# A gated linear-attention block: seven products for block 1's keys and queries, another sequence of the first half, late features for three blocks' queries, fewer GpSimd scale operations

## The chip, the cores and the metric

The kernel runs on one core of a Trainium2 chip. Its time is the device time of one execution in microseconds (us); lower is better. The core has a matrix engine (TensorE, PE in the profile), a vector engine (VectorE, DVE), an activation engine (ScalarE, ACT), a general engine (GpSimd, POOL) and DMA queues, here those of SyncE (SP) and of GpSimd. Each engine works through its own instructions in the order of the program and waits on semaphores for the others.

## The reference

```python
x = A_x                                   # 1 x 2048 x 512
xn = _layernorm(x, axis=-1)
s = _A_ref(xn, A_wqkv, A_wo)              # linear attention
g = _silu(_B_ref(xn, B_w1, B_w2, B_w3, B_w4))
return x + s * g

def _A_ref(x, wqkv, wo):                  # H = 32 heads of Dh = 16
    phi = lambda t: jnp.where(t > 0, t + 1, jnp.exp(t)) + 1e-6
    pq, pk = phi(q), phi(k)
    kv = jnp.einsum("bhsd,bhse->bhde", pk, v)
    z = jnp.einsum("bhsd->bhd", pk)
    num = jnp.einsum("bhqd,bhde->bhqe", pq, kv)
    den = jnp.einsum("bhqd,bhd->bhq", pq, z)[..., None] + 1e-6
    o = num / den
    return o.reshape(B, S, D) @ wo

def _B_ref(x, w1, w2, w3, w4):
    h = _gelu(_layernorm(x, axis=-1) @ w1)
    # four quarters of h shifted by +1, -1, +2, -2 rows, concatenated
    x1 = x + hs @ w2
    return x1 + _gelu(_layernorm(x1, axis=-1) @ w3) @ w4   # F = 1376
```

All of it is float32.

## The kernel before

**Tiling.** The 2048 rows are 4 blocks (b) of 512 rows, and each block is 4 tiles (i = 4b to 4b + 3) of 128 rows. The inner dimension of 512 is four chunks (c) of 128. A product in full precision is made of three products of rounded parts: each operand is split into a high part (`...h`, rounded) and a low part (`...l`, the rest), and high x high, high x low and low x high are added in PSUM (`products`, line 475). So every operand costs one rounding (mostly on ScalarE) and one subtraction (VectorE) ahead of its first product (`rounded`, line 483).

**First half.** For every tile: keys, their features (`feature_k`, line 774), the gram product of keys and normalized rows (`gram`, line 866, accumulated over all 16 tiles in four PSUM banks), queries and their features. For every block: the mixing products with W1 (`mixer`, tiles `h`, `ht`), the transforms of their result (`forms`) and the products with W2 (`mix2`, tiles `pam`, `pbm`, `pem`, `o`).

Keys and queries of a tile are made in one of two ways. `key` and `query` (lines 789 and 810) project one tile from the plain transposed rows: 12 products of 512 columns each, and a VectorE step that takes the mean out. `keys_queries(b, j)` (line 839) makes keys and queries of two tiles together in seven block products in place of eight (Winograd's scheme): 42 products of 512 columns for four projections. It needs the centred rows and four sums of them (`make_u`, line 672, for which the means of the block come back from DRAM as one broadcast row, `um`) and four sums of the key and query weights (`forms_kq`, line 819, named "T" in the sequence). Before, blocks 0 and 1 take the first way and blocks 2 and 3 the second.

**Queries' features.** phi needs max and exp of the query. `feature_q` (line 802) makes relu(q), exp(-relu(-q)) on ScalarE (two Relu and one Exp), stores the first part in DRAM (`pqd`) and adds the second by an accumulating DMA from GpSimd's queue. `turn_q` (line 1168) fetches the features in the second half, normalizes them on VectorE and sends them through a transposition.

**Scales.** The row statistics (`mv1`, `mv2`) become 1/sqrt(var + eps) by a power on GpSimd (`power`, line 598). The operations around it (add eps; the negative scale `ns1`; minus mean times scale, `nm1` and `nm2`; the variance of the second norm, `pu`) are GpSimd's too (`scale_x`, `scale_u`, `mixed`).

**Second half.** Per block, pairs of W3 blocks (`up_pair`, seven products, Gelu), the products with W4 (`down`, tiles `acc`), the attention output (`attend_pair`, tiles `pas`, `pbs`, `pes`) and the gate.

**What sets the order.** All operations are recorded in a plan (`Plan`, line 87). The order in which TensorE's operations are recorded gives each a nominal time from a table of costs; `deadlines` counts back from these to a due time of every other operation. `emit` (line 268) then places the operations of all engines in simulated time, with costs for each kind, and writes the program in that order; TensorE may take an operation up to 12 us ahead of its turn. `SOONER` (line 1510) moves the due times of single operations by quarters of a microsecond. So the sequence of the first half, `ORD` (lines 1382 to 1390), sets TensorE's order: "q", "k" are projections, ("kq", b, j) seven products, "g" a gram, "mix" a block's mixing, "m2" two tiles' W2 products, "w1" the centring and splitting of W1 (`w1_for`; its column mean comes from TensorE as `w1m`), "st" row statistics, "u" the centred forms, "x" scaled rows, "a" and "h" the broadcast rows (`abc`) and edges for mixing.

Of the kernel before, what the change touches and what calls it, by code (L numbers as in the profile page):

```python
# [13 lines left out]

P = 128
SCARCE = 3.0
EPS = 1e-5
# [69 lines left out]
class Plan:  # L87
# [70 lines left out]
    def act(self, out, src, func, scale=1.0, bias=None, total=None):  # L158
        nc = self.nc
        psum = out.tile.psum or src.tile.psum  # L160
        lat = .17 + out.n / 1200 + (.09 if isinstance(scale, View) else 0) + (0 if psum else .02)
        table = 0 if func == AF.Exp else 1 if func in (AF.Gelu_apprx_tanh, AF.Tanh) else None

        def emit():
            kw = {} if bias is None else {"bias": bias.get()}
            if total is not None:
                kw["accum_out"] = total.get()
            nc.scalar.activation(out.get(), src.get(), func, scale=get(scale), **kw)  # L168

        self.add("ACT", lat - .1, lat, [src, scale, bias], [out] + ([] if total is None else [total]), emit, table=table)  # L170

    def vec(self, eng, out, reads, emit, pair, scalars=0):
        views = [v for v in reads if isinstance(v, View) and v.n > 4]
        sb = not any(v.tile.psum for v in views + [out])
        n = max([v.n for v in views] + [out.n])
        if eng == "POOL":
            lat = (.3 if n <= 8 else .15 + n / (435 if pair else 1000))
# [219 lines left out]
def linear_attn_gated_by_mixer(  # L397
# [30 lines left out]
    SUMS = "DVE"  # L428
    SOON = {"T": 30.0, "u": 5.0}
    AHEAD = 70.0, 50.0, 30.0, 10.0, 0.0  # L430
# [14 lines left out]
    def piece(name, dt=F32):  # L445
        return pl.new("p", name, dt, PIECE)[:, :512]
# [151 lines left out]
    def power(out, src, n):  # L598
        nh = nhalf[:, :n]
        pl.add("POOL", .53 + .15 * n, .53 + .15 * n, [src, nh], [out],  # L600
               lambda: g.tensor_tensor(out.get(), src.get(), nh.get(), op=ALU.pow))  # L601
# [12 lines left out]
    def scale_u(b):  # L614
        p = small(f"pu{b}", QT).all
        pl.ts(p, var(mv1, b * QT, b * QT + QT), 1.0 + EPS, EPS * EPS, ALU.mult, ALU.add, eng="POOL")
        power(au[:, b * QT:b * QT + QT], p, QT)
# [75 lines left out]
    def split_halo(b):  # L693
        for c in range(NC):
            for o, q in ((0, 0), (BT + 2, 2)):
# [3 lines left out]
                mh, ml = (t[:, 2:4] for t in UT[b][c])  # L699
                pl.add("POOL", .25, .25, [v, mh], [hi], lambda hi=hi, v=v: g.tensor_copy(hi.get(), v.get()))  # L700
                pl.add("POOL", .25, .25, [v, hi, ml], [lo], lambda lo=lo, hi=hi, v=v: g.tensor_tensor(
                    lo.get(), v.get(), hi.f32.get(), op=ALU.subtract))
# [71 lines left out]
    def feature_k(i, ps, centred=False):  # L774
# [132 lines left out]

    HT, AH, BW = {}, {}, {}

    def mix1(b, g):  # L910
        ps = bank(f"h{b}_{g}")
        a = 2 + SHIFT[g]
        products(ps, [W1.chunk(c, g * P, (g + 1) * P) + ut(b, c, a, a + BT) for c in range(NC)])
        t = HT[b, ORDER.index(g)] = piece(f"ht{b}_{g}")
# [73 lines left out]
    def mixed(i, xv):  # L988
# [9 lines left out]
        w = small(f"w2{b}", QT).all  # L998
        pl.ts(w, var(mv2, a, z), EPS, None, ALU.add, eng="POOL")
        power(r, w, QT)  # L1000
        pl.tt(m, means(mv2, a, z), r, ALU.mult, eng="POOL")
        pl.ts(m, m, -1.0, None, ALU.mult, eng="POOL")
        for t in range(2):
# [315 lines left out]

    def stats_of(b, rows=True):  # L1320
        for j in range(QT if rows else 0):
            i = b * QT + j
# [4 lines left out]
        spread_m(b)  # L1327
        if rows:
            load_u(b, 1)
# [6 lines left out]

    def w1_for(b):
        if b == 0:
            W1.center(by_dma=True)
# [11 lines left out]

    KQ1 = False
    query(0)
    gram(0)
    query(1)
    load_u(1, 1)
    if KQ1:
        forms_kq()
    scaled(1)
    gram(1)  # L1360
    if KQ1:
        stats_of(1, False)
    query(2)
    gram(2)
    query(3)
    if KQ1:
        make_u(1)
    gram(3)
    pl.load(hal.all, halo.rearrange("p q c -> p (q c)"))
    scale_u(0)  # L1370
    spread_a(0)
    split_halo(0)
    if not KQ1:
        plain_u(1)
        key(4)
        scale_u(1)
    spread_a(1)
    W1 = Weights("w1", w1)
# [3 lines left out]
    if KQ1:  # L1382
        ORD = [("kq", 1, 0), ("w1", 0), ("st", 2), ("g", 4), ("kq", 1, 1), ("g", 6), ("g", 5), ("mix", 0), ("w2",), ("g", 7)]
    else:
        ORD = [("q", 4), ("w1", 0), ("k", 5), ("g", 4), ("q", 5), ("st", 2), ("k", 6), ("g", 5), ("mix", 0), ("q", 6), ("w2",), ("k", 7), ("g", 6), ("T",), ("q", 7), ("g", 7)]
    ORD += [("a", 2), ("h", 1), ("m2", 0), ("mix", 1), ("m2", 1), ("u", 2), ("m2", 4), ("m2", 5), ("x", 2),
# [3 lines left out]
    DO = {"x": scaled, "kq": keys_queries, "w1": w1_for, "st": stats_of, "g": gram, "mix": mixer, "w2": prepare_w2,  # L1390
          "a": spread_a, "h": split_halo, "m2": mix2, "u": make_u, "k": key, "q": query, "T": forms_kq}
# [51 lines left out]
    for b in range(NQ):  # L1443
# [66 lines left out]
    SOONER = (  # L1510
        36, 64, 186, 8, 199, 16, 1412, -8, 1489, 8, 1493, 41, 1549, 16, 1982, 4, 2419, -8, 2854, 16, 3165, 8,
        4113, -8, 4394, -8, 4725, 64, 4805, 16, 4810, 65, 4814, -32,
    )
# [39 lines left out]
```

## Time and profile before

| | us |
|---|---|
| median of 3 runs | 518.98 |
| the three runs | 520.24, 518.98, 516.49 |
| the profiled execution | 517.69 |
| its span, first to last instruction | 515.8 |

| stretch of the span | TensorE busy | VectorE busy | ScalarE busy | GpSimd busy |
|---|---|---|---|---|
| 0 to 60 us | 58.0 | 46.3 | 50.8 | 35.0 |
| 60 to 130 us | 69.7 | 62.5 | 50.5 | 19.3 |
| 130 to 230 us | 98.8 | 86.2 | 88.1 | 34.2 |
| 230 to 512 us | 281.0 | 216.7 | 148.5 | 16.1 |

The mean granted TensorE clock is 0.999. A row of the timeline names start, duration, engine, line, operation, what is written and read, shapes, and in brackets the idle time ahead and what ended it. Line numbers are mostly those of the helpers that record an operation (L147 products, L168 ScalarE, L190 and L200 VectorE), so the names of the tiles tell which step it is. TensorE's products overlap: one of 512 columns is shown with 0.39 us but the next starts after some 0.23.

### The profile page before, as it was taken

Reading aid. Unit: us, or ns where it says so; the run is one execution under the profiler, and the core shown is the slowest. Engines: PE = TensorE matmul, PEld = TensorE weight load, DVE = VectorE, ACT = ScalarE, POOL = GpSimd, SP = SyncE. Lnnn points to the kernel's source line nnn. Section 1 sums busy time; section 2 is a strip of 40 time slices with the busy share of each in tenths; the row PEclk is TensorE's granted clock in tenths of the full one; section 3 lists DMA queues with packets and bytes.
Section 4 is the critical chain, followed back from the end, with each engine's and each line's share of the span. In section 5 each row is a group of like instructions: output and inputs, shape, how many; then the busy total and the mean of one; then the engine's idle time right before and its main releaser. Section 6 shows DMA issues by size and latency. Waiting matters only on the chain.

```text
span 515.8 us, 8950 instructions
## 1 busy us (share of the span) xinstructions
PE 507.6 (98%) x2983; PEld 441.1 (86%) x2983; DVE 412.4 (80%) x832; ACT 337.9 (66%) x694; POOL 104.6 (20%) x191
## 2 busy tenths in 40 slices
PE   9999999999999999999999999999999999999996
PEld 7677788898778878898899989899898898999985
DVE  5987669999879996989999998655796659965545
ACT  5899778775979989878767644355443455643521
POOL 1589311244521732211100011000020000110000
PEclk9999999999999999999999999999999999999999
DMA  8978961989695999999875859577486594499404
GB/s 274 318 206 153 287 153 36 263 254 247 218 267 155 244 318 249 281 183 334 286 212 155 281 174 254 180 191 209 132 212 227 179 233 156 114 278 303 119 5 120
DMA packets 78194, 109.05 MB, mean 211 GB/s; under 512 B 8396, under 2 KB 31460, under 8 KB 78148
## 3 DMA queue, kind: packets, MB, share of 16 engines
q1 hardware_dynamic: 68788, 91.44, 55.5%
q0 software_dynamic: 9360, 17.04, 19.8%
q8 instruction: 23, 0.38, 0.3%
q14 instruction: 23, 0.19, 0.1%
HBM read 67.15 MB, written 32.91 MB: 194 GB/s over the span
## 4 chain that ended last, share of the span: by engine, by line
PE 77%; ACT 14%; DVE 3%; DMA 2%; issue 2%; POOL 1%; SPq 0%; ACTq 0%; DVEq 0%; POOLq 0%
PE acc L147 23%; PE pb L147 11%; PE pe L147 6%; PE pbs L147 4%; PE h L147 4%; PE g L147 4%; PE k L147 3%; PE pbm L147 3%; PE pa L147 3%; PE pes L147 2%; PE a L147 2%; ACT qe L168 2%; PE pbk L147 2%; PE q L147 2%; DMA o<-x 2%
## 5 line engine op out<-in xcount | busy, mean ns | idle before, releaser
L224 POOL DMA_DIRECT2D th<-in_x x14 | 12.4, 939 | 245.8 <-DVE th L200 108.5
L224 POOL DMA_DIRECT2D o<-x x16 | 14.6, 975 | 59.7 <-DVE o L190 47.3
L168 ACT ACTIVATE p<-pb 128x256 f32<-128x256 f32 x20 | 7.6, 382 | 27.3 <-PE pb L147 27.1
L190 DVE TENSOR_TENSOR gf<-pa,p 128x256 f32<-128x256 f32 x20 | 8.4, 418 | 18.8 <-PE pa L147 15.3
L168 ACT ACTIVATE th<-xo 128x512 f32<-128x512 f32 (+1 forms) x16 | 9.8, 620 | 20.0 <-DVE xo L190 19.9
L224 POOL DMA_DIRECT2D zacc<-kr x16 | 15.2, 949 | 36.8 <-DVE kr L200 22.7
L168 ACT ACTIVATE gf<-gf 128x512 f32<-128x512 f32 (+1 forms) x40 | 20.8, 523 | 0.8
L168 ACT ACTIVATE p<-pe 128x256 f32<-128x256 f32 x20 | 7.7, 384 | 17.5 <-PE pe L147 17.5
L224 POOL DMA_DIRECT2D pqd<-qe x16 | 14.8, 927 | 20.4 <-DMA pqd<-qr 8.8
L190 DVE TENSOR_TENSOR xo<-acc,xo 128x512 f32<-128x512 f32 (+1 forms) x16 | 10.4, 670 | 10.6 <-PE acc L147 9.6
L190 DVE TENSOR_TENSOR gf<-u,pe 128x256 f32<-128x256 f32 x20 | 8.3, 417 | 9.9 <-PE pe L147 9.8
L168 ACT ACTIVATE y<-o,nm,rs 128x512 f32<-128x512 f32 x16 | 12.1, 803 | 3.4 <-POOL nm L195 3.4
L168 ACT ACTIVATE ht<-ht 128x512 f32<-128x512 f32 x16 | 9.7, 626 | 6.5 <-DVE ht L190 6.4
L200 DVE SCALAR_TENSOR_TENSOR kr<-kt,kr 128x512 f32<-128x512 f32 x16 | 10.9, 683 | 3.7 <-ACT kt L168 3.6
L190 DVE TENSOR_TENSOR ht<-h,abc 128x512 f32<-128x512 f32 x16 | 10.7, 680 | 3.4 <-PE h L147 3.4
L168 ACT ACTIVATE x<-x,nm,rs 128x512 f32<-128x512 f32 x16 | 12.8, 810 | 0.0
L168 ACT ACTIVATE u<-pb 128x256 f32<-128x256 f32 x20 | 7.7, 384 | 6.0 <-PE pb L147 6.0
L200 DVE SCALAR_TENSOR_TENSOR th<-th,so 128x512 f32<-128x512 f32 (+1 forms) x17 | 10.9, 653 | 0.5
L200 DVE SCALAR_TENSOR_TENSOR pq<-pq,rd 128x512 f32<-128x512 f32 x16 | 11.0, 687 | 0.2
L601 POOL TENSOR_TENSOR rs<-w,nhalf 128x4 f32<-128x4 f32 (+2 forms) x10 | 10.7, 1074 | 0.7
L200 DVE SCALAR_TENSOR_TENSOR qz<-pq,zb 128x512 f32<-128x512 f32 x16 | 10.7, 685 | 0.2 <-DMA pq<-pqd 0.2
L168 ACT ACT_TABLE_LOAD x8 | 10.3, 1283 | 0.9 <-PEq L1544 0.8
(1682 smaller groups left out, 2239.1 us busy)
## 6 DMA issues: line engine op xcount, KB each, us to landing
w_s<-in_w SPq DMA_DIRECT2D x28, 256.0 KB, 4.7
x<-in_x SPq DMA_DIRECT2D x16, 256.0 KB, 3.5
zacc<-kr POOLq DMA_DIRECT2D x16, 256.0 KB, 5.1
pqd<-qr SPq DMA_DIRECT2D x16, 256.0 KB, 3.2
pqd<-qe POOLq DMA_DIRECT2D x16, 256.0 KB, 6.7
o<-x POOLq DMA_DIRECT2D x16, 256.0 KB, 6.3
x1d<-o SPq DMA_DIRECT2D x16, 256.0 KB, 5.7
pq<-pqd SPq DMA_DIRECT2D x16, 256.0 KB, 3.5
```

The source lines that it names most:

```text
L147: lambda: nc.tensor.matmul(out.get(), lhs.get(), rhs.get(), start=start, stop=stop, skip_group_check=more))
L168: nc.scalar.activation(out.get(), src.get(), func, scale=get(scale), **kw)
L190: self.vec(eng, out, [a, b], lambda: self.e(eng).tensor_tensor(out.get(), a.get(), b.get(), op=op), True)
L200: lambda: self.nc.vector.scalar_tensor_tensor(out.get(), a.get(), get(s), b.get(), op0=op0, op1=op1),
L224: lambda: self.nc.gpsimd.dma_start(out.get(), get(src), accum_op=ALU.add), mb=mb)
L601: lambda: g.tensor_tensor(out.get(), src.get(), nh.get(), op=ALU.pow))
```

## The change

- The sequence: block 1 no longer goes through `key` and `query`; its keys and queries come from ("kq", 1, 0) and ("kq", 1, 1), behind a `make_u(1)`. `forms_kq` ("T"), the centring of W1 and block 0's mixing move ahead of them. The loads of block 1's rows, the edges and W1 are steps of `ORD` now. The variable `KQ1` and its branches go.
- Late features: for tiles from `LATE` = 4 on, `feature_q` only stores the raw query, and `turn_q` makes the features in the second half: Relu and Exp on ScalarE, and one step min(exp, 1) + relu on VectorE.
- Scales: the operations around the power go from GpSimd to VectorE; minus mean times scale is one step (`negative_mean`); `ns1` is made for block 0 alone.
- The key features' rounding adds its constant as an immediate (Copy) in place of a tile (Identity).
- The planner's costs of ScalarE and GpSimd operations, `SOON` and `SOONER` get other values.

```diff
@@ costs
-        lat = .17 + out.n / 1200 + (.09 if isinstance(scale, View) else 0) + (0 if psum else .02)
+        lat = (.15 if psum else .195) + out.n / 1200
+        lat += .092 * (isinstance(scale, View) + isinstance(bias, View)) + (.095 if total is not None else 0)
...
-    SOON = {"T": 30.0, "u": 5.0}
+    LATE = QT
+    SOON = {}
@@ scales
+    def negative_mean(out, mv, a, z, r):
+        pl.stt(out[:, a:z], means(mv, a, z), -1.0, r, ALU.mult, ALU.mult)
...
-        pl.ts(w, var(mv1, lo, lo + n), EPS, None, ALU.add, eng="POOL")
+        pl.ts(w, var(mv1, lo, lo + n), EPS, None, ALU.add)
         power(r, w, n)
-        pl.ts(ns1[:, lo:lo + n], r, -1.0, None, ALU.mult, eng="POOL")
-        pl.tt(nm1[:, lo:lo + n], means(mv1, lo, lo + n), ns1[:, lo:lo + n], ALU.mult, eng="POOL")
+        negative_mean(nm1, mv1, lo, lo + n, r)
+        if lo < LATE:
+            pl.ts(ns1[:, lo:lo + n], r, -1.0, None, ALU.mult)
...
@@ features
-        pl.act(hi, r, AF.Identity, bias=tiny.all)
+        pl.act(hi, r, AF.Copy, bias=TINY)
...
     def feature_q(i, t):
+        if i >= LATE:
+            pl.soon(pl.store(pqd[i].all, t))
+            return
...
     def turn_q(i):
-        pl.fetch(pq, pqd[i].all)
+        if i < LATE:
+            pl.fetch(pq, pqd[i].all)
+        else:
+            v, r = piece(f"qv{i}"), piece(f"qr{i}")
+            pl.fetch(v, pqd[i].all)
+            pl.act(by_block(r), by_chunk(v), AF.Relu, scale=col(rs1, i))
+            pl.act(by_block(pq), by_chunk(v), AF.Exp, scale=col(rs1, i))
+            pl.stt(pq, pq, 1.0, r, ALU.min, ALU.add)
...
@@ sequence
-        ORD = [("q", 4), ("w1", 0), ("k", 5), ("g", 4), ("q", 5), ("st", 2), ("k", 6), ("g", 5), ("mix", 0), ("q", 6), ("w2",), ("k", 7), ("g", 6), ("T",), ("q", 7), ("g", 7)]
-    ORD += [("a", 2), ("h", 1), ("m2", 0), ("mix", 1), ("m2", 1), ("u", 2), ("m2", 4), ("m2", 5), ("x", 2),
...
+    ORD = [
+           ('lu',), ('q', 0), ('hal',), ('x', 1), ('q', 2), ('lw',), ('g', 0), ('h', 0), ('st', 1), ('g', 2),
+           ('a', 1), ('q', 1), ('u', 1), ('h', 1), ('g', 1), ('q', 3), ('a', 0), ('g', 3), ('w1', 0), ('T',),
+           ('w2',), ('mix', 0), ('kq', 1, 0), ('kq', 1, 1), ('st', 2), ('g', 6), ('h', 2), ('a', 2), ('g', 5),
+           ('x', 2), ('u', 2), ('st', 3), ('g', 4), ('mix', 1), ('g', 7), ('m2', 0), ('a', 3), ('m2', 1),
+           ('w1', 2), ('m2', 4), ('kq', 2, 0), ('m2', 5), ('x', 3), ('g', 10), ('kq', 2, 1), ('mix', 2), ('u',
+           3), ('w1', 3), ('g', 8), ('g', 9), ('m2', 8), ('kq', 3, 0), ('kq', 3, 1), ('m2', 9), ('g', 11),
+           ('g', 12), ('g', 14)
+           ]
...
```

More of the change, by code (lines that the diff above doesn't have):

```diff
@@ L176, in vec @@
         if eng == "POOL":
[L177 removed]
+            lat = (.4 if n <= 8 else .15 + n / (435 if pair else 1000))
             return self.add(eng, lat, lat, reads, [out], emit, two=n > 64)
@@ L912, in mix1 @@
         a = 2 + SHIFT[g]
-        products(ps, [W1.chunk(c, g * P, (g + 1) * P) + ut(b, c, a, a + BT) for c in range(NC)])
+        products(ps, [HELD[0].chunk(c, g * P, (g + 1) * P) + ut(b, c, a, a + BT) for c in range(NC)])
         t = HT[b, ORDER.index(g)] = piece(f"ht{b}_{g}")
@@ L998, in mixed @@
         w = small(f"w2{b}", QT).all
-        pl.ts(w, var(mv2, a, z), EPS, None, ALU.add, eng="POOL")
+        pl.ts(w, var(mv2, a, z), EPS, None, ALU.add)
         power(r, w, QT)
-        pl.tt(m, means(mv2, a, z), r, ALU.mult, eng="POOL")
-        pl.ts(m, m, -1.0, None, ALU.mult, eng="POOL")
+        negative_mean(nm2, mv2, a, z, r)
         for t in range(2):
@@ L1318, in plain_u, with stats_of @@
             rounded(*(t[:, 2:2 + BT] for t in UT[b][c]), XT[b, c])
-    def stats_of(b, rows=True):
-        for j in range(QT if rows else 0):
+    def stats_of(b):
+        for j in range(QT if b > 1 else 0):
             i = b * QT + j
@@ L1327, in stats_of @@
         spread_m(b)
-        if rows:
+        if b > 1:
             load_u(b, 1)
@@ L1350, in w1_for, with halos, load_w1 @@
                     pl.fetch(W1.hl[c][n].f32, W1D[:, (2 * c + n) * 512:(2 * c + n + 1) * 512])
[L1352 to L1378, printed above, removed]
     early_s, early_f = EARLY
     fill = [lambda f=f: make_w4(f) for f in early_f] + [lambda s=s: make_pair(s) for s in early_s]
-    if KQ1:
-        ORD = [("kq", 1, 0), ("w1", 0), ("st", 2), ("g", 4), ("kq", 1, 1), ("g", 6), ("g", 5), ("mix", 0), ("w2",), ("g", 7)]
-    else:
-        ORD = [("q", 4), ("w1", 0), ("k", 5), ("g", 4), ("q", 5), ("st", 2), ("k", 6), ("g", 5), ("mix", 0), ("q", 6), ("w2",), ("k", 7), ("g", 6), ("T",), ("q", 7), ("g", 7)]
-    ORD += [("a", 2), ("h", 1), ("m2", 0), ("mix", 1), ("m2", 1), ("u", 2), ("m2", 4), ("m2", 5), ("x", 2),
[3 rows of a table removed]
-    DO = {"x": scaled, "kq": keys_queries, "w1": w1_for, "st": stats_of, "g": gram, "mix": mixer, "w2": prepare_w2,
+    ORD = [
[7 rows of a table added]
+           ]
+    def halos():
+        pl.load(hal.all, halo.rearrange("p q c -> p (q c)"))
+        scale_u(0)
+    def load_w1():
+        HELD.append(Weights("w1", w1))
+    DO = {"lu": lambda: load_u(1, 1), "hal": halos, "lw": load_w1, "x": scaled, "kq": keys_queries, "w1": w1_for, "st": stats_of, "g": gram, "mix": mixer, "w2": prepare_w2,
           "a": spread_a, "h": split_halo, "m2": mix2, "u": make_u, "k": key, "q": query, "T": forms_kq}
```

16 lines of the change are left out of this document (8 added, 8 removed), and 6 rows, old and new, of tables (ORD, SOONER).

## The prediction

> **What bounds the kernel now.** I read the page first, then the windows of 20 us, then the waits and single stretches of the timeline. The page (span, busy time, chain of waits):
>
> ```profile
> span 515.8 us, 8950 instructions
> ...
> PE 507.6 (98%) x2983; PEld 441.1 (86%) x2983; DVE 412.4 (80%) x832; ACT 337.9 (66%) x694; POOL 104.6 (20%) x191
> ...
> PE 77%; ACT 14%; DVE 3%; DMA 2%; issue 2%; POOL 1%; SPq 0%; ACTq 0%; DVEq 0%; POOLq 0%
> ```
>
> TensorE is busy for 98% and carries 77% of the chain; 17% pass through ScalarE and VectorE. Where those two are full is told by the windows (busy us in the order PE, PEld, DVE, ACT, POOL):
>
> ```profile
> 0.00:20.00 20.00, 18.70 (x70) 13.94 (x71) 14.21 (x29) 12.90 (x26) 4.58 (x19) 1.00 0.89 314
> 20.00:40.00 20.00, 19.52 (x84) 15.08 (x83) 17.44 (x38) 20.00 (x38) 16.00 (x33) 1.00 0.76 202
> ...
> 80.00:100.00 20.00, 20.00 (x109) 16.95 (x108) 20.00 (x38) 15.92 (x28) 4.33 (x5) 1.00 0.59 143
> ...
> 400.00:420.00 20.00, 20.00 (x128) 17.92 (x127) 13.17 (x28) 10.51 (x25) 0.00 (x0) 1.00 0.65 193
> ```
>
> ScalarE is full from 20 to 40 us, VectorE from 80 to 100; late in the span neither limits anything. A busy TensorE isn't yet TensorE at its rate, so I take the rate from starts in the timeline, and then look for its waits:
>
> ```profile
> 39.74 0.39 PE L147 MATMUL g<-k3h,x3h 128*128 128x512 f32 x1
> ...
> 42.30 0.40 PE L147 MATMUL g<-k3h,x3l 128*128 128x512 f32 x1
> 42.53 0.27 PE L152 MATMUL ab<-ident,au 128*4 128x128 f32 x1
> ...
> 42.88 0.40 PE L147 MATMUL k<-wk_0l,u_0h 128*128 128x512 f32 x1
> ```
>
> ```profile
> PE pbk L147 <- DVE ht L190: 0.5, 1, 0.5
> PE pbk L147 <- ACT p1k L168: 0.4, 1, 0.4
> ```
>
> Eleven steps of a gram group take 42.30 - 39.74 = 2.56 us, so 0.233 us for a product of 512 columns. The longest waits inside the stream are these two of half a microsecond. So only two things can move the end: fewer columns through TensorE, and stalls that come or go.
>
> **Part by part.** The page's run took 517.69 us, of which the span is 515.8; the median of the three runs is 518.98, 1.29 above. I sum against 517.69.
>
> *Seven products.* Block 1 had four key and four query projections of 12 products, 96 of 512 columns. Now it is two calls of 42, so 84: 12 x 0.233 = 2.8 us less, all on the path. Block 1's means are now spread too, one more small transpose; from 42.53 to 42.88 it and the product behind it took 0.35 instead of 0.233, so +0.1. Sum -2.7.
>
> *W1 earlier.* In the changed order block 0's mixing products (h) stand right behind block 0's four grams, and the centring of W1 (w1m, then four corrections and four splits on VectorE) just ahead of them, with two gram products between. Before, w1m ran here:
>
> ```profile
> 48.33 0.40 PE L147 MATMUL w1m<-w1mh,onesr 128*128 128x512 f32 x1
> ```
>
> and the chain of waits shows h, with three more rows that are used below:
>
> ```profile
> 5.06 9.52 PE k L147 x34
> 14.59 0.86 PE ksum L147 x2
> ...
> 63.57 11.19 PE h L147 x48
> ...
> 86.73 0.71 PE pam L147 x6
> ```
>
> VectorE's prices (timeline, and a group of half-width sums) and ScalarE's (timeline):
>
> ```profile
> 20.39 0.21 DVE L195 TENSOR_SCALAR sx<-sx 128x1 f32<-128x1 f32 x2
> ...
> 50.35 1.28 DVE L200 SCALAR_TENSOR_TENSOR w_s<-w1m,w_s 128x512 f32<-128x512 f32 x2
> ```
>
> ```profile
> L190 DVE TENSOR_TENSOR hs1f<-ht,ht 128x256 f32<-128x256 f32 x8 | 3.4, 422 | 1.3 <-ACT ht L168 1.1
> ```
>
> ```profile
> 205.20 0.62 ACT L168 ACTIVATE w_s1h<-w_sf 128x512 fp32r<-128x512 f32 x1
> 205.84 1.28 ACT L168 ACT_TABLE_LOAD   x1
> 207.14 1.15 ACT L168 ACTIVATE ht<-ht 128x512 f32<-128x512 f32 x2
> ```
>
> The 63.57 - 48.33 = 15.2 us of cover shrink to 2 x 0.233 = 0.5. The first correction (half of 1.28) and the rounding on ScalarE (0.62) with their handovers are about 1.5 us, so about 1.0 us of TensorE is idle there. If the mixing products of the first chunk can run ahead while the rest arrives, 0.5; if VectorE is late with its eight full-width steps, 1.6. I take +1.0.
>
> *VectorE in the first 100 us.* Two full-width steps in 1.28 us with 0.04 to spare on either side of the overlap make 0.60 to 0.64 a step; I take 0.60. Two of one column take 0.21, so 0.08 is a fair price for the small ones, and 0.42 less the same overlap is 0.34 for half width. Up to the first sum of block 0's mixing result (o<-pam) its queue held 97 full, 18 half and 20 small operations: 58 + 6 + 2 = 66 us, and TensorE came to that product at 86.73. In the changed order the same point has 127, 31 and 39: 76 + 11 + 3 = 90 us, since block 1's forms, the weights of its seven products and all mixing products of blocks 0 and 1 now stand ahead of it. TensorE gets there after 368 products of 512 columns (85.7), 12 of 256 (1.4 at half the price), four slow ones (0.86 each) and six transposes (0.6), counted from 5.06: 96.2 us. VectorE cannot start at zero: it idled 6.1 us in the first window and 2.6 in the second (20 less 13.94 and 17.44). 90 + 8.7 = 98.7, so it is 2.5 us behind TensorE where it had some 12 to spare (86.73 - 66 - 8.7). Part of the 2.5 is the 1.0 above and waits that TensorE has there anyway. I take +1.2; the ends are 0 (VectorE waits less for ScalarE) and 3.
>
> *GpSimd's scale operations.* 34 tiny operations leave GpSimd and 27 join VectorE, as nm becomes one step and later blocks need no ns. Most of the 27 are the small ones already in the 90. New are the handovers VectorE to GpSimd (the power) and back to VectorE (nm): in VectorE's queue splits and features stand behind such an nm, and ScalarE's x waits for it.
>
> ```profile
> L601 POOL TENSOR_TENSOR rs<-w,nhalf 128x4 f32<-128x4 f32 x7 | 8.0, 1149 | 0.5
> L168 ACT ACTIVATE qe<-qe 128x512 f32<-128x512 f32 x16 | 9.7, 621 | 0.0
> L168 ACT ACTIVATE qe<-qt,ns 128x512 f32<-128x512 f32 x8 | 5.7, 711 | 0.0
> L168 ACT ACT_TABLE_LOAD x8 | 10.3, 1283 | 0.9 <-PEq L1544 0.8
> ```
>
> I cost it at nothing: VectorE has other work queued between asking and using, and a power is 1.15 us. Without that cover it is 1.15 a time, at most twice on the path. Perfetto Trace Analysis of the Trainium skill (Optimizing Scalar/DVE Operations) says that moving work between GpSimd and VectorE might not help, as they share a port. By it the move gains nothing; no row here shows what it would gain, and the sum has nothing for it either.
>
> *Late features.* Twelve query tiles lose two Relu and one Exp of ScalarE (12 x (0.71 + 0.71 + 0.62) = 24.5 us) and one accumulating DMA of GpSimd in the first half; one Relu, one Exp and one step of VectorE (0.60) come back past 300 us, where a window of 20 us has 13.17 of VectorE and 10.51 of ScalarE in it. Block 1's extra roundings and PSUM copies (10 x 0.62) take a quarter of the relief back. ScalarE, and VectorE behind it, so get slack past 120 us, where TensorE waited for p1k and ht. The two waits are 0.9 us. They may stay, or a little over twice that may go (a modelled end hides part of a wait): 0 to -2.0. I take -1.0.
>
> *Table loads.* The 12 late Exps stand among Gelus: ten more loads of 1.28 us, all past 300 us. Each pair of loads encloses the first PSUM copies of the next group, behind the last Gelu of the one before:
>
> ```profile
> 313.02 0.38 ACT L168 ACTIVATE gf<-pb 128x256 f32<-128x256 f32 x1
> 315.08 0.38 ACT L168 ACTIVATE p<-pb 128x256 f32<-128x256 f32 x1 [1.68 <-PE pb L147]
> ```
>
> The idle 1.68 us there now hold 1.28 + 0.62 (an Exp), so the copy is 0.2 late; TensorE wants the bank back 12 products of 256 columns later (1.4 us), and the copy takes 0.38. Hidden, with some 0.8 to spare. I take +0.2 over five such places; 0 to 1.
>
> Sum: -2.7 + 1.0 + 1.2 - 1.0 + 0.2 = -1.3, so 516.4 us. VectorE is next in line behind TensorE.
>
> **Rivals.** *The first half gets smooth (513.0).* ScalarE's 18 us of net relief leave TensorE no stall in the first 216 us: -2.7, the waits at their most (-2.0), and the new stalls hidden: -4.7. Against it: VectorE's 90 us.
>
> *VectorE held by a landing (521.4 or 526.4).* Block 1's means come back as a broadcast (um) while VectorE stands at about 41 us of its queue, and the mixing rows (abc) soon after. Behind the subtraction of um are queued the split of w1m and the corrections and splits of W1, so the mixing products, and with 0.5 us of cover TensorE waits in full.
>
> ```profile
> L218 SPq DMA_DIRECT2D um<-mrow x2: 416/433/450, 91.0 to 139.7; - x2
> ...
> DMA to landing us min/median/max: 4.6/4.6/4.6
> ```
>
> ```profile
> wo_s<-in_wo SPq DMA_DIRECT2D x4, 256.0 KB, 9.6
> ```
>
> At 4.6 us it lands in time; at the 9.6 that other transfers took it is 5.0 us late. VectorE has no slack up to 100 us, so that isn't made good: 516.4 + 5.0 with one late landing, + 10 with both. It decides from about 3 us of lateness on.
>
> *The switches cost more (519.9).* By the rows a load takes 1.28 us and the next operation starts 0.02 after it (205.84, 207.14). If a switch also drained ScalarE for about its own length, the copy would be 1.5 late with 0.8 to spare, 0.7 x 5 = 3.5 more. ScalarE: Activation LUTs of the Trainium skill (What ACT_TABLE_LOAD costs) gives 1283 ns and 1380 ns of drain, 2.66 us a switch. The trace agrees with the first and shows no gap for the second.
>
> **The numbers.** Forecast 516.4 with 0.56, smooth first half 0.19, VectorE held 0.14 (half of it twice), dear switches 0.11. The range goes from 512.5 to 521.5: the forecast's own ends (517.7 - 2.7 + 0.5 - 2.0 = 513.5, and 517.7 - 2.7 + 1.6 + 3 + 1 = 520.6), the dear switches, one late landing and most of the smooth case; left out are the double loss and a tail on either side. The three runs of before lie 0.7% apart, so 1% is about what can be told from no change. From 518.98 that is 513.8 and 524.2: faster 0.19 (the smooth case), slower 0.08 (the double loss and a little), same 0.73.
>
> **What would show it.** Right: 12 fewer products of 512 columns; VectorE busy for nearly all of 40 to 100 us; TensorE's first h waits about 1 us for W1's corrections or roundings; no wait of TensorE for the copies (p) past 300 us. Wrong: VectorE waiting for um or for GpSimd's powers between 30 and 50 us; TensorE waiting for p behind a table load; or no wait at all at h. The forecast falls if TensorE loses over 3 us between 40 and 75 us.

## The result and the profile after

The changed kernel takes 512.6 us (median of five executions, 511.97 to 514.09) against 517.61 for the kernel before; the ratio is 0.990, 95% interval 0.986 to 0.993. Run again among the experiments it gave 512.7 and 0.990 (0.988 to 0.992). The forecast was 516.4, the rival "the first half gets smooth" 513.0. The times of the kernel before lie in two groups near 517.4 and 519.3 us, in shares that differ by chip (nine of eleven in the upper group on the chip of e1 to e4, a third to under a half on the others), so its median moves between 517.5 and 519.2.

The page of the profiled execution (512.43 us): span, busy time, chain of waits, and the group of the table loads.

```profile
span 510.7 us, 8948 instructions
...
PE 502.9 (98%) x2972; PEld 437.9 (86%) x2972; DVE 426.3 (83%) x885; ACT 348.9 (68%) x703; POOL 91.2 (18%) x145
...
PE 86%; DVE 5%; ACT 5%; DMA 2%; issue 1%; SPq 1%; DVEq 0%; ACTq 0%
...
L170 ACT ACT_TABLE_LOAD x18 | 23.1, 1283 | 1.1 <-PEq L1543 0.8
```

ScalarE's share of the chain fell from 14% to 5% and TensorE's rose from 77% to 86%. Now TensorE's waits (in all, times, longest), and the windows of 20 us where the forecast saw VectorE full:

```profile
PE h L148 <- ACT w_0h L170: 1.3, 1, 1.3
PE warm L148 <- POOL ones L511: 1.0, 1, 1.0
PE pbs L148 <- ACT u2s L170: 0.3, 1, 0.3
```

```profile
40.00:60.00 20.00, 18.71 (x81) 14.81 (x80) 19.89 (x38) 16.90 (x30) 15.41 (x32) 1.00 1.05 277
60.00:80.00 20.00, 19.93 (x85) 14.96 (x84) 19.34 (x42) 16.88 (x29) 2.80 (x3) 1.00 0.53 170
80.00:100.00 20.00, 20.00 (x101) 16.79 (x100) 19.95 (x45) 15.58 (x34) 7.39 (x9) 1.00 0.50 119
100.00:120.00 20.00, 20.00 (x138) 18.46 (x137) 19.98 (x47) 11.78 (x25) 11.20 (x19) 1.00 0.78 187
```

VectorE is over 96% busy from 40 to 120 us, as foretold, and one wait of TensorE is left that is longer than 0.3 us once the warming products are done: that of the first mixing product.

The listed waits don't add up to the gain, so I measured **lateness**: the start of a product in the trace less 5.06 us (the start of the first one in the kernel before) and less TensorE's own work ahead of it, which is 0.2325 us for each product of 512 columns, half for 256, 0.85 for a slow one, 0.11 for each row of the other small ones (a product of `kv` is two such rows, 0.11 apart). All work together is 2.7 us less after than before. Lateness in us, by the time at which a product would start without it, that is 5.06 plus the own work ahead (the last column is the last product; e-numbers are experiments below):

| due by (us) | 20 | 40 | 50 | 62 | 140 | 200 | 230 | end |
|---|---|---|---|---|---|---|---|---|
| before | 1.0 | 2.0 | 2.5 | 2.6 | 3.9 | 6.3 | 7.3 | 12.4 |
| after | 0.0 | 0.0 | 1.5 | 2.1 | 3.0 | 3.4 | 3.7 | 9.6 |
| after, a second profile (e11) | 2.9 | 2.8 | 4.3 | 4.9 | 5.8 | 6.1 | 6.4 | 11.7 |
| e1 no shifts | 1.3 | 2.0 | 3.8 | 3.8 | 5.0 | 5.4 | 5.8 | 11.4 |
| e4 old sequence | 1.1 | 2.7 | 3.0 | 3.1 | 4.2 | 4.9 | 5.2 | 11.4 |
| e5 before, no shifts | 1.0 | 2.6 | 2.6 | 2.6 | 3.8 | 7.6 | 8.8 | 15.4 |
| e9 sequence alone | 1.2 | 1.9 | 5.7 | 6.7 | 8.6 | 9.7 | 10.2 | 16.4 |
| e10 late features alone | 1.3 | 2.6 | 2.6 | 2.6 | 3.5 | 4.8 | 5.2 | 11.2 |
| e17 scales alone | 1.3 | 2.9 | 3.2 | 3.3 | 4.2 | 8.4 | 9.4 | 15.4 |

So up to the last product 2.7 us come from columns and 2.8 from lateness: 2.0 at the start, 3.1 between 62 and 230 us (4.7 became 1.6), less 1.5 at the first h and at block 1's products (0.6 became 2.1 from 40 to 62 us) and 0.8 in the second half (5.1 became 5.9). Only differences are read from the second half: its 1270 products of 256 columns start 0.118 us apart and are counted at 0.116, some 2 us in all. The expectations below count a product of `kv` as one row, so the losses up to 230 us that they name are 1.8 to 2.0 higher (6.7 for 4.7).

Of the waits listed for the kernel before, three lie between 60 and 230 us, 1.2 us in all:

```profile
PE pbk L147 <- DVE ht L190: 0.5, 1, 0.5
PE pbk L147 <- ACT p1k L168: 0.4, 1, 0.4
PE pbm L147 <- DVE o L190: 0.3, 1, 0.3
```

### The profile page after: what moved, and what is told of

Same layout as the page of the kernel before. It is cut to its first block, busy times and chain, and to the rows that moved or that the text cites. A ratio compares the mean times of both kernels' runs of the same rounds, so it can differ in the third digit from the quotient of the medians.

```text
span 510.7 us, 8948 instructions
## 1 busy us (share of the span) xinstructions
PE 502.9 (98%) x2972; PEld 437.9 (86%) x2972; DVE 426.3 (83%) x885; ACT 348.9 (68%) x703; POOL 91.2 (18%) x145
## 4 chain that ended last, share of the span: by engine, by line
PE 86%; DVE 5%; ACT 5%; DMA 2%; issue 1%; SPq 1%; DVEq 0%; ACTq 0%
PE acc L148 23%; PE pb L148 11%; PE h L148 8%; PE g L148 7%; PE pbk L148 6%; PE pe L148 5%; PE pbm L148 4%; PE pbs L148 4%; PE pek L148 3%; PE pa L148 3%; PE pem L148 2%; PE a L148 2%; PE pes L148 2%; DMA y_1t<-y_1d 2%; PE pak L148 1%
## 5 line engine op out<-in xcount | busy, mean ns | idle before, releaser
L226 POOL DMA_DIRECT2D zacc<-kr x16 | 13.9, 867 | 40.6 <-DMA zacc<-kr 22.2
L604 POOL TENSOR_TENSOR rs<-w,nhalf 128x4 f32<-128x4 f32 (+2 forms) x10 | 10.1, 1012 | 35.5 <-DVE w L197 32.6
L598 DVE BATCH_NORM_STATS2 st<-o 128x6 f32<-128x512 f32 x16 | 10.9, 686 | 3.5 <-DMA o<-x 3.4
L202 DVE SCALAR_TENSOR_TENSOR pq<-pq,qr 128x512 f32<-128x512 f32 x12 | 8.1, 683 | 4.1 <-ACT pq L170 4.0
```

Source lines behind the costliest of these rows:

```text
L202: lambda: self.nc.vector.scalar_tensor_tensor(out.get(), a.get(), get(s), b.get(), op0=op0, op1=op1),
L226: lambda: self.nc.gpsimd.dma_start(out.get(), get(src), accum_op=ALU.add), mb=mb)
L598: pl.add("DVE", .62, .69, [xv], [st], lambda: nc.vector.bn_stats(st.get(), xv.get()))
```

## The experiments

Each kernel was timed in several rounds beside the kernel before on its chip. Kernels of different chips are compared by their ratios to it; 0.002 is 1.0 us. But its median is 519.2 on the chip of e1 to e4 and 517.5 to 518.0 on the others, so the ratios of e1 to e4 come out up to 0.003 lower beside those of other chips. Where that matters, the difference of the medians in us stands beside the ratio. Chips: e1 to e4 one, e5 to e8 another, e9 to e16 a third, e17 and e18 a fourth. e6, e9, e10, e14 and e17 have the immediate constant of the key features too.

| | sequence | features | costs | scales on | shifts | median us | ratio, 95% |
|---|---|---|---|---|---|---|---|
| before | old | early | old | GpSimd | its own | 517.6 | 1 |
| after | new | late | new | VectorE | its own | 512.6 | 0.990 (0.986 to 0.993) |
| e1 | new | late | new | VectorE | none | 514.15 | 0.991 (0.989 to 0.993) |
| e2 | new | early | new | VectorE | none | 514.48 | 0.991 (0.989 to 0.993) |
| e3 | new | late | new | GpSimd | none | 513.85 | 0.990 (0.988 to 0.992) |
| e4 | old | late | new | VectorE | none | 516.21 | 0.994 (0.993 to 0.996) |
| e5 | old | early | old | GpSimd | none | 520.78 | 1.004 (1.003 to 1.006) |
| e6 | old | early | new | GpSimd | none | 517.69 | 0.999 (0.998 to 1.001) |
| e7 | new | late | old | VectorE | none | 514.88 | 0.992 (0.990 to 0.994) |
| e9 | new | early | old | GpSimd | none | 517.86 | 0.999 (0.998 to 1.001) |
| e10 | old | late | old | GpSimd | none | 516.98 | 0.997 (0.996 to 0.999) |
| e14 | new | early | new | GpSimd | none | 516.27 | 0.997 (0.996 to 0.999) |
| e17 | old | early | old | VectorE | none | 519.93 | 1.004 (1.002 to 1.005) |

**e1, the shifts.** They count recorded operations, so no kernel with another count can keep them; e1 is the base.

```diff
-            ahead=6.0, table=SOONER)
+            ahead=6.0)
```

> The changed kernel with the list of due-time shifts (SOONER) empty; everything else stays. It is the base of the next kernels, since the list counts operations and can't be kept when one is added. Theories: (A) beside the 12 products, the gain comes from the late features, which relieve ScalarE and GpSimd between 60 and 230 us; (B) it comes from the other sequence; (C) it comes from the tuned shifts and from the scale operations leaving GpSimd. A and B: 512 to 513.5, no stretch of TensorE's lateness moves by more than 0.5. C: 514.5 to 516, with TensorE's small waits back between 60 and 230 us.

0.9908 against 0.9896 is 0.6 us, within the uncertainty; the medians differ by 1.5 (514.15 and 512.6), and 514.15 lies between the two ranges of the expectation. The stretch from 62 to 230 us loses 2.0, in the changed kernel 1.6: of theory C the part on this stretch falls. What the shifts are worth otherwise, 0.6 to 1.5 us and mostly ahead of 50 us, isn't told apart from the start, where two profiles of the changed kernel differ by 2.9.

**e2, early features for all tiles.**

```diff
-    LATE = QT
+    LATE = S // P
```

> As e1, but features of all 16 query tiles are made in the first half (LATE = 16): 24 Relu, 12 Exp and 12 accumulating DMAs come back there, and the 12 Relu, 12 Exp and 12 VectorE steps past 300 us go. A: TensorE's lateness between 60 and 230 us grows by 2.4 + 0.8 = 3.2 us (what it fell from before to after), and the second half gives back 0.8, so e1 + 2.4. B or C: the first half stays as in e1 and the second gives back 0.8, so e1 - 0.8.

Only 0.3 slower than e1 where A wanted 2.4. Beside the rest of the change the late features bring next to nothing. From 230 us on, e2 loses 5.9 and e1 5.6: the 12 late Exps and ten more table loads cost nothing that can be seen.

**e3, the scale operations back on GpSimd.**

```diff
-        pl.ts(w, var(mv1, lo, lo + n), EPS, None, ALU.add)
+        pl.ts(w, var(mv1, lo, lo + n), EPS, None, ALU.add, eng="POOL")
...
```

> As e1, but the operations around the powers are GpSimd's again as in the kernel before (negative scale for all blocks, minus mean times scale in two steps). A and B: e1 within 0.6; my sum has nothing for this part. C: e1 + 1.5 or more, with VectorE or ScalarE waiting for the scales in the first 60 us, where GpSimd was busy for 35 of 60 us before.

0.3 faster than e1, which is no difference. C's half about the scale operations falls.

**e4, the old sequence** under all else that is new (`ORD` of before, 96 single products for block 1).

> As e1, but with the sequence of the kernel before: block 1 by 96 single products, the centring of W1 far ahead of block 0's mixing, query 0 and then gram 0 at the start; late features and VectorE's scales stay. A: columns +2.8 - 0.1, the wait at the first h gone (-1.4), the start-up waits back (+1.9), and the stretch from 60 to 230 us as in e1: e1 + 3.2. B: that stretch is also as in the kernel before, + 3.2 more: e1 + 6.4. C: as A.

2.1 slower, of which 2.7 are columns; 62 to 230 us loses 2.1 as in e1 (2.0). So the sequence isn't what took the losses out of that stretch (B falls), but neither were the late features by e2. The parts had to be tried on the kernel before.

**e5 to e7, the planner's costs.** e5 is the kernel before without its shifts; e6 adds the new costs; e7 is e1 with the old ones. The diff of e7:

```diff
-        lat = (.15 if psum else .195) + out.n / 1200
-        lat += .092 * (isinstance(scale, View) + isinstance(bias, View)) + (.095 if total is not None else 0)
+        lat = .17 + out.n / 1200 + (.09 if isinstance(scale, View) else 0) + (0 if psum else .02)
...
-        pl.add("POOL", POW + .17 * n, POW + .17 * n, [src, nh], [out],
+        pl.add("POOL", .53 + .15 * n, .53 + .15 * n, [src, nh], [out],
```

> The kernel before with its own list of due-time shifts empty, as the base for e6. e4 has the same sequence and products, yet TensorE lost 2.0 us instead of 3.8 between 62 and 200 us and 2.3 instead of 2.9 from there to 230. Theories: (D) the planner's new costs place ScalarE's and VectorE's work better there; (A2) the late features do, but only beside the single projections of the old sequence; (E) the shifts of the kernel before bought its start at the price of that stretch. D and A2: 62 to 230 us as before (6.7) or worse, and 1 to 2 us lost up to 60 us, so the time is that of before + 1 to + 2. E: 62 to 230 us falls to about 4.3 and the time is that of before within 1.

> e4 with the early features and GpSimd's scale operations back, so e5 with nothing but the planner's new costs (and the constant as an immediate in the key features' rounding). D: as e4 within 0.8, and faster than e5 by 2 or more, with 62 to 230 us at 4.3 of lateness. A2: as e5 within 0.8, and slower than e4 by about 2.4. E: e4, e5 and e6 within 1 of each other.

> e1 with the planner's costs of the kernel before (ScalarE's, GpSimd's small operations, the powers). D: e1 + 2 or more, lost between 62 and 230 us. A2 and E: e1 within 0.8.

The shifts of before were worth 2.1 us (1.004; 2.8 by the medians), so the kernel before had part of its losses tuned away already, and E falls. The new costs alone bring e5 - 3.1, more than D asked, but e6 stays above e4, by 0.0047 (2.4 us, the number of A2) in the ratios and by 1.5 in the medians: costs do part, and late features with VectorE's scales, the two things that e4 has besides, another. Where the costs gain isn't shown: the profiled execution of e6, 519.5 us, isn't typical of the others, as TensorE waits 1.8 once, and the clock falls behind it, of which more below. In the new kernel the costs are worth 0.8 (0.9923 and 0.9908).

**e9, e10, e17: one part alone on e5.** e9 has the new sequence, e10 `LATE = QT`, e17 the scale operations on VectorE.

> e7 with early features and GpSimd's scale operations: of the whole change only the sequence (block 1's seven products with it) and the immediate constant stay, with the planner's old costs and no due-time shifts. Its base is e5. Theories: (S) the sequence alone takes TensorE's losses out of the stretch from 62 to 200 us (5.2 in e5), and late features and costs have nothing left to do there: that stretch at 2 to 2.5, the time that of e7 within 0.8, so 5 to 6 under e5. (J) the parts are needed together: that stretch at 4 or more, e7 + 2 or more.

> e5 with the late features (and the immediate constant) and nothing else of the change: the old sequence, the planner's old costs, GpSimd's scale operations, no shifts. If ScalarE's features are what makes the copies (p5m, p1k) late that TensorE waits for between 140 and 200 us in e5 (1.4 and 0.9): e5 - 2 to - 3.5, that stretch from 3.8 to 1 or less. If only the order of the plan decides: e5 within 0.8.

> e5 with the scale operations on VectorE and nothing else of the change (but the immediate constant): old sequence, early features, the planner's old costs, no shifts. If ScalarE's wait for GpSimd's nm at 140 us (3.1 in e5) is the cause of what TensorE loses there: that wait goes, TensorE's 3.8 between 140 and 200 us falls to 1.5 or less, and the time is e5 - 2 to - 3.5. If ScalarE's load is the cause: e5 within 1, the losses stay. If VectorE's 27 operations and the handovers cost: e5 + 0 to + 2.

TensorE's waits from 60 to 230 us in e5, in e10 and in e17:

```profile
PE pem L147 <- ACT p5m L168: 1.4, 2, 1.1
PE pbk L147 <- ACT p1k L168: 0.9, 1, 0.9
PE pbk L147 <- DVE p5k L190: 0.2, 1, 0.2
```

```profile
PE pem L148 <- ACT p5m L169: 0.6, 1, 0.6
```

```profile
PE pem L148 <- ACT p5m L169: 1.2, 2, 0.8
PE pem L148 <- DVE u2k L191: 0.6, 1, 0.6
PE pbm L148 <- ACT p1m L169: 0.3, 1, 0.3
```

Late features alone are worth 0.0067 (1.004 to 0.9973), 3.5 us: from 140 to 200 us e5 loses 3.8 and e10 1.3. The scale operations alone are worth nothing that can be told (1.0036; the medians differ by 0.9). That rules out what the timelines of ScalarE in e5 and then in e17 suggested:

```profile
143.56 2.94 ACT L168 ACTIVATE y<-o,nm,rs 128x512 f32<-128x512 f32 x4 [3.06 <-POOL nm L195]
```

```profile
141.63 2.94 ACT L169 ACTIVATE y<-o,nm,rs 128x512 f32<-128x512 f32 x4 [1.00 <-DVE nm L201]
```

ScalarE's wait for nm falls from 3.06 to 1.00 us, yet TensorE loses 4.2 from 140 to 200 us instead of 3.8: a long wait of an engine off the path, just ahead of the loss, was not its cause. The sequence alone (e9) brings 2.4 us by the ratios, about its columns; its stretch from 62 to 200 us loses 3.0, between S and J, and it pays for a wait of 2.0 at h.

**e14, sequence and costs without late features.** Early features, and the scale operations on GpSimd.

> The new sequence and the planner's new costs; features of all tiles in the first half, the scale operations on GpSimd, no shifts (e1 without its late features and without VectorE's scales). Overlap (each of late features and costs takes the same losses of TensorE, and what the second one finds is gone): as e1, e2 and e3 within 0.8, a ratio of 0.990 to 0.992 to the kernel before. Addition (late features are worth 3.8 wherever ScalarE makes features): e3 + 2 or more, 0.994 or more.

Above e3 by 3.5 us in the ratios (0.997, 0.9903) and by 2.4 in the medians, with late features as the only difference, where e2 and e1 differed by 0.3. From 80 to 100 us TensorE loses 2.2, e3 0.2. The waits of TensorE from 5 to 500 us and of all engines from 70 to 100 us name it:

```profile
PE pbm L148 <- ACT p1m L170: 1.4, 1, 1.4
```

```profile
DVE w_f L192 <- DMA pqd<-qe: 2.0, 1, 2.0
ACT w_t4h L170 <- DVE w_f L192: 1.3, 1, 1.3
```

VectorE waits 2.0 us for a buffer until an accumulating DMA of query features has landed; ScalarE and TensorE follow. These DMAs stand in GpSimd's queue among the scale operations. Take away either (late features in e3, scales on VectorE in e2) and the wait is gone: neither pure overlap nor addition.

**e8, e12, e13: the wait at the first h.** e8 sums W1 in two chains and records its centring earlier; e12 gives four of the weights' sums to GpSimd and keeps the shifts; e13 lengthens the wait.

```diff
@@ e8
-                for c in range(1, NC):
-                    pl.gather(t, self.src[:, c])
+                t2 = piece(self.name + "t2")
+                pl.load(t2, self.src[:, 2])
+                pl.gather(t, self.src[:, 1])
+                pl.gather(t2, self.src[:, 3])
+                pl.tt(t, t, t2, ALU.add)
...
-           ('q', 3), ('a', 0), ('g', 3), ('w1', 0), ('T',),
+           ('w1', 0), ('q', 3), ('a', 0), ('g', 3), ('T',),
@@ e12
-            pl.tt(t[0][c], q[c], k[c], ALU.subtract)
+            pl.tt(t[0][c], q[c], k[c], ALU.subtract, eng="POOL")
...
-            pl.tt(t[2][c], q[c + 2], q[c], ALU.subtract)
+            pl.tt(t[2][c], q[c + 2], q[c], ALU.subtract, eng="POOL")
...
-    SOON = {}
+    SOON = {"T": 20.0}
@@ e13
                 ts = rounds(self.name + "m")
+                t2 = piece(self.name + "t2")
+                pl.act(t2, t, AF.Copy)
+                pl.ts(t, t2, 1.0, None, ALU.mult)
```

> e1 with W1's column sum made of two loads and two accumulating DMAs side by side and one VectorE addition (in place of one load and three accumulations one behind the other), and the centring of W1 recorded ahead of query 3, so that some 22 products stand between w1m and the first h in place of 2. If the wait at the first h is for want of cover and the last accumulation sets when w1m can run: the wait (1.6 to 1.8 us in e1) goes, VectorE's step costs at most 0.6, so e1 - 1.0 to - 1.8. If VectorE's queue up to there is what is late (the rival of my prediction, 90 us of work): the wait moves to the next h or to the seven products of block 1, and the time is that of e1 within 0.5.

> The changed kernel itself, beside e9, e10 and e12 on one chip. Against e1 the shifts of SOONER should be worth 0.6 (by the ratios to the kernel before) to 1.8 (by TensorE's lateness at the end, 13.4 and 11.65).

> The changed kernel, with its shifts, but four of the eight sums of the key and query weights (the first two and the fifth and sixth) on GpSimd, which waits for the second accumulation of W1 from 10 to 16 us, and the tiles of that step free to be taken 20 us earlier. If VectorE's queue (full from 40 to 60 us, and the holder of TensorE in e8) is what the wait at the first h comes from: 2.4 us less on it, so the wait of 1.3 goes: e11 - 1.0 to - 1.8. If VectorE and GpSimd slow each other at full width (in e3 a GpSimd cast of two columns took 3.33 us beside a busy VectorE): e11 + 0.5 to + 3. If W1's last accumulation alone sets that wait: e11 within 0.5.

> e1 with two more steps in W1's column sum ahead of w1m (a copy by ScalarE, a copy back by VectorE, 0.61 and 0.35 us with two handovers), so that the wait at the first h grows from 1.6 to 2.6 to 2.8. If the clock is halved for some 3 us after a wait of about 1.8 or more: a row of the windows just behind with a granted clock near 0.5, products at 0.43 in place of 0.233 for about eight of them, so e1 + 1.1 + 1.6 = + 2.7, and a mean clock of 0.994. If the clock has nothing to do with the wait: e1 + 1.1.

e8 took 515.5 us (0.9935), slower than e1. The wait at h is gone, and TensorE waits for VectorE at block 1's first product instead (timeline of TensorE, then windows of 2 us; the number third from the end of a window is the granted clock):

```profile
54.14 0.40 PE L148 MATMUL h<-u_3h,w_3l 128*128 128x512 f32 x1
56.40 0.47 PE L148 MATMUL pbk<-wk_0h,u_0h 128*128 128x512 f32 x1 [1.86 <-DVE ht L192]
...
58.63 0.63 PE L148 MATMUL pek<-kq_0h,us_0h 128*128 128x512 f32 x1
59.05 0.63 PE L148 MATMUL pek<-kq_0l,us_0h 128*128 128x512 f32 x1
```

```profile
54.00:56.00 2.00, 0.54 (x3) 0.10 (x1) 2.00 (x4) 0.84 (x2) 1.97 (x4) 1.00 1.05 403
56.00:58.00 2.00, 1.60 (x5) 1.35 (x6) 2.00 (x5) 1.99 (x3) 1.88 (x8) 0.73 1.08 336
58.00:60.00 2.00, 2.00 (x6) 1.52 (x6) 2.00 (x6) 1.37 (x4) 1.99 (x1) 0.50 1.10 265
60.00:62.00 2.00, 2.00 (x10) 1.60 (x9) 1.92 (x5) 1.96 (x4) 0.57 (x1) 0.91 1.10 263
```

VectorE is busy for the whole of 54 to 60 us, so its queue is what TensorE meets there; earlier centring only moves the place of the wait. And the wait has an after-effect: the clock halves, and products start 0.42 apart (58.63, 59.05) instead of 0.233; lateness grows by another 1.6 us. e11 is level with e1 by ratio (0.990, 0.991) and 1.5 under it in the medians. e12 took 516.88 (514.31 to 518.57): slower than e11, though its profiled execution is the quickest of the twelve and still waits 1.1 at h. So giving GpSimd those sums doesn't pay. Three of the twelve (517.52 to 518.57) have a mean clock of 0.994, as in e13; what the others lost was in no profile and stays open. e13 took 518.21 and splits: seven of twelve executions have a mean clock of 0.994 or 0.995 and take 518.2 to 519.1, the other five 0.997 to 1.000 and 515.9 to 517.2. In every profile the clock falls to half once TensorE has no more work, and that alone makes means of 0.997 to 1.000; 3.41 us at half clock on top take off another 0.003. So the lengthened wait brings the after-effect more often than not, though not in the profiled execution (516.41 us). The rest above e1 is more than the 1.1 expected, as lateness also grows by 1.5 between 80 and 100 us.

**e15, e16, e18: towards a better version.** e15 makes block 0's features late too; e16 adds GpSimd's scales and W1's centring ahead of gram 3; e18 makes block 0's features at about 135 us instead and takes over the shifts but those on W1.

```diff
@@ e15
-    LATE = QT
+    LATE = 0
@@ e16
-           ('q', 3), ('a', 0), ('g', 3), ('w1', 0), ('T',),
+           ('q', 3), ('w1', 0), ('a', 0), ('g', 3), ('T',),
@@ e18
+    def features(b):
+        for i in range(b * QT, b * QT + QT):
+            v, r, e = (piece(f"q{n}{i}") for n in "vre")
+            pl.fetch(v, pqd[i].all)
+            pl.act(by_block(r), by_chunk(v), AF.Relu, scale=col(rs1, i))
+            pl.act(by_block(e), by_chunk(v), AF.Exp, scale=col(rs1, i))
+            pl.stt(e, e, 1.0, r, ALU.min, ALU.add)
+            pl.soon(pl.store(pqd[i].all, e))
```

> e1 with block 0's features made late too (LATE = 0): 8 Relu, 4 Exp and 4 accumulating DMAs less in the first 50 us, where ScalarE was full from 40 to 50, and 4 Relu, 4 Exp and 4 VectorE steps more in the second half, with up to 8 table loads. If ScalarE holds the start (k1h, w_0h): e1 - 0.5 to - 1.5. If it is VectorE and the cover of w1m: e1 within 0.5, or + 0.5 to + 1 where the first block of the second half can't hide the loads.

> e15 with the scale operations on GpSimd again (27 small operations less on VectorE) and the centring of W1 recorded 10 products earlier, ahead of gram 3: cover of 2.8 us instead of 0.5 for the first h. If VectorE's queue was what moved the wait to block 1's seven products in e8: the wait at h goes and none appears there, e15 - 1 to - 1.6, and with it less than the changed kernel. If GpSimd's small operations are late beside a busy VectorE (u_0l in e3): a wait of 1 to 2 us at h stays, e15 within 0.5, or + 1.6 more if it passes 1.8.

> e16 with block 0's features made in the middle of the first half (fetched back at about 100 to 130 us, one Relu, one Exp and one VectorE step for each tile, stored again) in place of the second half, and with the shifts of the changed kernel but those on W1's centring. e16 lost 2.7 us between 260 and 300 us where block 0's late features met a full VectorE, and 1.6 less than e1 up to the first products of block 1. If both hold: e16 - 2.3 to - 2.7 by the features, - 0 to - 1.3 by the shifts, so 511.3 to 513.0, under the changed kernel or level with it. If four VectorE steps in the first half are as dear as in the second (VectorE full up to 120 us): e16 - 0 to - 1.

515.84 (0.997), 515.34 (0.995) and 515.73 us (0.996): none beats the changed kernel. e16 does lose the wait at h (lateness 2.3 at 50 us, 3.8 in e1), so with VectorE relieved the cover works; but e15 and e16 lose 2.6 us between 260 and 300 us, where e1 loses 0.8. The window of e16, and TensorE's waits from 230 to 310 us:

```profile
260.00:280.00 20.00, 19.23 (x123) 16.84 (x123) 19.61 (x41) 11.98 (x30) 0.00 (x0) 1.00 0.64 184
```

```profile
PE pbs L148 <- DVE so L192: 0.4, 1, 0.4
PE pbs L148 <- DVE m_t2l L192: 0.3, 1, 0.3
```

VectorE is full there, and TensorE waits for its results (so, m_t2l): four more steps have no room. e18 avoids that and falls into the other hole: its features ran here,

```profile
133.81 0.72 ACT L170 ACTIVATE qr<-qv,rs 128x512 f32<-128x512 f32 x1
...
139.68 0.71 ACT L170 ACTIVATE qe<-qv,rs 128x512 f32<-128x512 f32 x1
```

and lateness grows from 4.9 to 8.0 between 140 and 200 us, as in e5 (3.8 to 7.6; in e16 3.9 to 4.5). With eight operations of ScalarE and four of VectorE put back just ahead of that stretch its loss is back; e18 has shifts as well, which e16 hasn't, and their part wasn't tried apart.

## Why the forecast was wrong

- **Seven products, -2.7: right.** The program's own work is 2.7 us less.
- **W1 earlier, +1.0: right in place and cause.** TensorE waits 1.3 for w_0h; from 40 to 50 us it loses 1.5 where it lost 0.5 before.
- **VectorE in the first 100 us, +1.2: right in kind, too large.** VectorE is over 96% busy to 120 us and holds TensorE by 0.6 from 50 to 62 us. e8 shows it as the bound: what is gained at h is lost at block 1's products.
- **GpSimd's scale operations, 0: right** (e3, e17), with one condition the sum didn't see: beside early features they hold the accumulating DMAs and through them a buffer of VectorE (e14).
- **Late features, "0 to -2.0. I take -1.0": the step that failed.** It was the only term that took losses of TensorE away. I read their worth off two listed waits, 0.9 us, and capped it at a little over twice. From 62 to 230 us TensorE lost 4.7, most of it in gaps that the list leaves out (it has 1.2 there); after the change it loses 1.6, so 3.1 went where the sum had 1.0. Late features alone are worth 3.5 (e10), and that on a kernel without shifts; those of before had taken 1.5 of that stretch's losses already (6.2 in e5).
- **Parts summed one by one: the second fault.** Late features and costs overlap: 3.5 and 3.1 alone on e5, but 0.3 and 0.8 as the last part put in. I had nothing for the costs, and gave no reason. Which one carries the gain inside the changed kernel is therefore no question with an answer. Beside VectorE's scale operations each suffices for most of it (e2 without late features 514.48, e7 without the costs 514.88, e1 with both 514.15); beside GpSimd's the costs don't (e14, 516.27).
- **Table loads, +0.2 (and the rival of dear switches): nothing** (e2), and no wait of TensorE for p. The second half's 0.8 isn't theirs; before's shifts are a candidate (e5 loses 6.6 there, before 5.1), not tested further.
- **The start was not in the sum.** It gave 2.0 us in the profile shown. About half is lost from 20 to 40 us and may go with the sequence and the shifts: 1.0 to 1.6 in the profiles with the old sequence, 0 to 1.2 in those with the new one, nothing in the two of the changed kernel. The other half is luck of the execution: TensorE's first product starts at 4.62 us in place of 5.06, but in e11, the same kernel (514.53 us), only at 5.68, behind a wait of 0.9 for the first weights, and the slow products then take 0.85 a row in place of 0.43 until 10.06 us, so TensorE is 2.9 late there.
- **VectorE held by a landing: didn't come.** The subtraction of um follows without idle time at 39.00 us.

The rival of the smooth first half (0.19) has the right number, 513.0, and half of the account: relief and the planner's costs did more than the waits "at their most" (3.1 for 2.0), but the new stalls were not hidden (1.5 up to 62 us), and the start, which is in no rival, made up for them. So the number is in part luck.

## What to carry to other kernels

Before pricing a relief, compute the lateness of the bounding engine from starts and own work, stretch by stretch: a list of waits showed 1.2 us where 4.7 were lost. Check its prices on the trace, too: one product shown as two rows and counted once adds a loss that isn't there. Parts that relieve the same engine in the same stretch aren't additive; price them together, against a base without its fine tuning. And where the next engine in line is full, more work of TensorE ahead of one wait only moves it.

## What the hardware showed

- **A wait of about 2 us can halve TensorE's clock, if most of it falls into one step of the clock's record.** Waits of 1.8 (e6), 1.86 (e8) and 2.0 us (e9) were followed by 3.41 us at 0.5, which costs 1.5 to 1.6; waits of 1.3 (after) and 1.6 (e1) were not, nor were 1.9 in e15's and 2.1 in e13's profile. The traces tell these apart. In all twenty the granted clock changes only at multiples of 3.41 us from the record's first entry, which lies between 3.9 and 10.1 us. Cut into such steps, a step at full clock with up to 1.6 us of TensorE busy was followed by half clock in 23 of 24 cases (among them the end of every profile), one with 1.7 or more never. The waits of e13 and e15 were divided between two steps. So where the step's edge falls decides, and that differs by execution: two of ten executions of e15 and seven of twelve of e13 show the lower mean clock. The Trainium skill (TensorE: Matmul & The Clock Gate, Part 1) says that the clock goes to half after at least one idle window of about 3.4 us. The half rate agrees (0.42 apart); the idle time needed doesn't: a gap of 2.26 us between starts (54.14 to 56.40) was enough. TensorE's wait in e9, and steps of e9 and of e13 (the first number behind the comma is TensorE's busy time):

```profile
PE h L148 <- ACT w_0h L169: 2.0, 1, 2.0
```

```profile
42.26:45.68 3.42, 1.40 (x6) 0.83 (x6) 3.38 (x7) 3.42 (x7) 3.01 (x9) 1.00 1.07 262
45.68:49.09 3.41, 3.41 (x9) 2.63 (x9) 3.41 (x7) 3.41 (x8) 3.22 (x6) 0.50 0.65 168
...
41.75:45.16 3.41, 1.97 (x9) 1.27 (x7) 3.41 (x6) 3.41 (x8) 3.31 (x5) 1.00 1.08 210
45.16:48.58 3.42, 2.78 (x12) 2.30 (x13) 3.42 (x7) 3.42 (x8) 3.25 (x7) 1.00 1.00 272
```

- **A tiny operation of GpSimd can take 3 us beside a full VectorE.** In e3 a cast of two columns, 0.17 to 0.68 us elsewhere in that stretch, took 3.33 while VectorE was busy without a gap. It is no single case: of 1300 operations on such edge columns in the twenty profiles 116 took over 1 us, and in 115 of them VectorE was busy for over 90% of the time. A busy VectorE isn't enough, though: 417 of the 486 that took under 0.3 us ran beside one too. The cast shown ends at 42.96, as VectorE comes to steps that read w1m from PSUM (42.92), and the next ones, beside these steps, take 0.17 to 0.20. That it matters where VectorE's operands lie would fit, but wasn't tested.

```profile
39.63 3.33 POOL L706 CAST u_1h<-hal 128x2 fp32r<-128x2 f32 x1
```
